# A list of steps made anew, with fillers only into idle PSUM banks

## The chip, the cores and the metric

The kernel runs on one core of one Trainium2 chip. The metric is the device time of one execution in microseconds (us). The core has a matrix engine (TensorE, PE in the profile, with its weight loads as PEld), a vector engine (VectorE, DVE), a scalar engine (ScalarE, ACT), GpSimd (POOL) and a queue engine (SyncE, SP) that only issues DMAs here. TensorE writes into PSUM, which has eight banks; VectorE and ScalarE read it from there.

## The reference

Two blocks follow each other. The first is a delta-rule recurrence over 768 steps for 4 batches of 8 heads with a state of 48 x 48 each:

```python
k_n = k / (np.linalg.norm(k, axis=-1, keepdims=True) + 1e-06)
for t in range(S):
    y[:, :, t] = np.einsum('bhd,bhde->bhe', q[:, :, t], state)
    v_old = np.einsum('bhde,bhd->bhe', state, kt)
    state = state + bt[:, :, :, None] * np.einsum('bhd,bhe->bhde', kt, vt - v_old)
```

Its output, with the heads side by side (4 x 768 x 384), goes through a layer norm and a two-layer MLP with a residual:

```python
xn = (x - mu) / np.sqrt(var + 1e-06) * g_ln
ch = np.maximum(xn @ w_ch1, 0.0) @ w_ch2
return (x + ch).astype(np.float32)
```

All is 32-bit floating point. The first weight is 384 x 1536, the second 1536 x 384.

## The kernel before

The 768 steps are cut into 12 chunks of 64. Within a chunk the recurrence becomes matrix products: a Gram matrix of the keys (`gram`, products L821, copies L842 by ScalarE, then a DMA to DRAM named `gd`), the inverse of a triangular matrix made from it, a product of that inverse with the corrected values (`recur`, L1035 and L1059 or L1090; for chunk 0 L1071), the output (L1097) and the new state (L1107). For chunk 0 the inverse is made on TensorE (`first_inverse`): after one multiply by -beta (L745) come five stages, each with two products E (L773, one per half of the heads, 32 small matmul records each), a predicated copy of them by VectorE (L778), two products Z (L788), and then VectorE's transposes (L737) and ScalarE's copies (L731) of Z. For the later chunks the inverse is made by rows on VectorE (`rows_inverse`, pairs of L909 and L916), between a read of the Gram blocks from DRAM and a write and read of the result through DRAM, and two halves are joined on TensorE (L946, L951, L983, L989). Keys and queries of the first chunks are transposed on TensorE (`first_kt`, L630, with ScalarE's copies L635).

Each chunk's output goes through a layer norm (L1141 to L1153, the root on ScalarE at L1147), is transposed (L1185 for the first chunks), and enters the MLP of that chunk (`mlp`). Chunk 0 takes the plain form: 24 tiles of the first layer (L1408, six matmul records each, relu by ScalarE at L1416) and then the second layer (L1450). Chunk 1 uses L1428; later chunks use a form with fewer products (L1309) and the second layer a form with seven products (L1525). The weights arrive as 64-bit words that ScalarE, VectorE and GpSimd turn into 32-bit floats (L586, L591, L594, L604) in the start of the run.

All of it is recorded first as steps, each with its engine, an estimated cost, a function that issues it and the keys it reads and writes (`Line.add`), from which its dependencies follow. A long text `ORDER` then lists the numbers of all steps, and `Line.emit` issues them in that order; `in_this_order` makes every engine keep it. An `f` in the list is a filler: one matmul of a zeroed tile `nought` with 256 columns, whose result nobody reads (`zeros`, L1603, two matmul records), written always into the upper half of the PSUM tile f0. There are 21 of them, all ahead of the MLP's first tile. Three more fillers are ordinary steps: `fill` (L619), 512 columns each, into the PSUM tile f3 at the very start. The PSUM tiles are `two` and `by` (two banks each) and f0 to f3 (one bank each).

Of the kernel before, what the change touches and what calls it, by code (L numbers as in the profile page):

```python
# [16 lines left out]
C = 64  # L17
# [32 lines left out]
class Step:  # L50
    __slots__ = ("eng", "cost", "fn", "deps", "n", "name", "key", "plan")


class Line:
# [6 lines left out]
    def __init__(self):  # L61
        self.steps = []
        self.filler, self.fill_after = None, ()
        self.writer = {}
        self.readers = {}
        self.tag = "first"

    def add(self, eng, cost, fn, r=(), w=(), name="", after=(), **plan):
        s = Step()
        s.eng, s.cost, s.fn, s.n, s.name, s.plan = eng, cost, fn, len(self.steps), name, plan  # L70
        s.key = f"{self.tag} {eng} {name or next(k if isinstance(k, str) else k[0] for k in w)}"
        deps = set()
        for k in r:
            if k in self.writer:
                deps.add(self.writer[k])
        for k in (*w, *after):
            if k in self.writer:
                deps.add(self.writer[k])
            deps.update(self.readers.get(k, ()))
        for k in r:  # L80
            self.readers.setdefault(k, []).append(s)
        for k in w:
            self.writer[k] = s
            self.readers[k] = []
        deps.discard(s)
        s.deps = deps
        self.steps.append(s)
        return s

    def emit(self, tc):  # L90
# [6 lines left out]
        made = tc.nc.cur_bb.bb.instructions  # L97
        for w in ORDER.split():
            if w == "f":
                self.filler[0]()  # L100
                continue
            a, b = (w.split("-") * 2)[:2]
            for s in self.steps[int(a) : int(b) + 1]:
                assert s not in done and s.deps <= done, s.key
                n = len(made)
                s.fn()
                done.add(s)
                if s.eng == "DVE" and s.plan.get("port"):
                    shared = made[-1]
                if s.eng == "Pool" and "bulk" not in s.plan and shared is not seen:  # L110
                    tc.add_manual_dep(
                        made[n], shared.name,
                        mybir.DependencyInfo(mybir.DependencyClass.Sync, mybir.DependencyReason.DATA),
                        reason="shared port",
                    )
                    seen = shared
# [15 lines left out]
66 8 47 257 6 9-11 1 12 41-44 48-49 7 13 15 0 5 2 65 60 39 256 40 55 53-54 56 52 58-59 57 64 86 85 79 35 78 80 37-38  # L132
77 70 96 75 81 89 74 90 88 91 33 97 87 71 3 14 16 98-100 32 101 26 4 17 105-106 73 72 82 104 84 50 18 23 83 102 92
313 63 108 36 107 69 250 124-125 30 129 216 103 29 93-95 126 109-112 51 76 118-119 122 128 27 31 120 19 f f 133 115
130 114 410 314 409 404 401 113 316 411 315 406 68 407 261 264 403 67 327 260 263 262 265 414 328 266 413 259 326
408 325 412 131-132 134 230 121 123 127 f f 141 135 117 248 144 116 238 209-210 20 142 21-22 136 143 137 24-25 239
147-148 249 138 146 139 145 140 149 234 246 151 156 154 150 231 28 152-153 157 251 163 244 228 160 213 226 155 161
224 215 214 164 211-212 158-159 f f f f f 165 162 232 240 168 172 166-167 45 61 662 62 664 217 241 169-170 174 220
178 317 180-181 319 218 171 173 175-176 245 182 247 179 177 f 183 185 318 369 190 267 415 320 184 227 219 191 196
222 363 321-322 195 370 34 268-271 221 46 258 229 272 193 186 273 187 f 197 329 189 188 323 331 194 192 274-281 198  # L140
282 f f 330 199 283 200 284-285 235 286-289 223 290-291 f 201 205 242 236 243 332 364 333 206-208 203-204 202
334-335 339 337 292-294 665 233 225 237 666 661 674 676 416 400 338 f 341 343 371 254 340 295-299 345 300-303 346 f
361 372 362 349 365 350 366 f f 435 342 344 351 347 434 437 436 252 f 438 253 348 439 355 405 324 336 402 304 476
474 477 309 475 312 306 308 791 307 310 790 305 311 793 367-368 473 352 356 373 357-358 353 374 255 354 f f 440 575
359 577 360 478 576 601 578 581 602 376 607 579 582 375 479-481 418 585 419 580 586 387 420 608 583 589 584 590 587
593 421 417 482 399 678 668 484-485 442 486-496 382 588 594 377 379 597 591-592 613 595 388 381 596 598 422 497 423
378 498 424-425 614 428 599 603-604 426-427 619 675 663 667 677 673 679-680 380 609 394 600 620 429 605 638 431 441
610 430 433 393 432 443 606 383 389 444-445 611 615 499 669 483 500-510 681 511-515 390 516-517 384 518-519 448 446
639-640 447 385 616 612 391 449-450 397 670-671 395 1075-1076 1088 392 386 453 451-452 520 454 521 621 617 522-524
396 1078 398 469 1077 1080 1079 1087 924-925 795 792 788 794 796-797 787 525 798 526 672 682 618 683 641 623 642 624  # L150
643-645 625-626 646 627-628 647-648 629-630 527-528 653 529-530 458 622 455 531 456 532-533 457 461 799 534-535 654
536 459 537-541 460 542-543 659 544 465 631-634 649 684 689 687 932 688 686 928 931 545-547 655 934 548 926 690-693
463 462 466 468 464 467 550 552 551 549 933 936 1181 1184 1182 935 1183 938 937 656 694 697 650 829 833 685 696 789
471 1081-1082 635 800 698 830 801 835 699-701 834 836 839 831 841 840 842 702-704 657 705-709 803 710-711 553
712-714 802 554 557 832 555 558 556 847-848 837-838 715 1083 716-717 564 718 658 719 660 720-721 1550 1549 1089 856
930 1552 1090 853-855 559 862 843 563 561 560 562 804 565 722-725 939 726 845 805 566 844 808 810 809 846 568 567
569 813-814 811 863 806 864-867 859-860 470 807 812 818-819 727-728 857 869 940 868 815 729 851 849-850 852 941 730
820 731 816 732 817 733-736 570 825 942 821 571 574 573 822 826-827 823-824 828 572 879 889 880 872-873 881-883
874-875 884 943 1551 1554 858 870 737 944 738-745 695 746-759 945-946 1179 1187 651 1180 652 636-637 1189 1186 927
1191 929 1190 1188 1193 760 1192 876 890-892 877 947-949 1084-1085 1092 1091 1093 1555 1094 861 871 888 886-887 893  # L160
878 897-900 1095 885 901 894-895 1096 902 980 472 1194 903 1097 915 896 972 950-951 981 764 762 1086 1098 761 763
1100 1195 904-905 916 906-909 975 917-918 910 982 986 973 978 1562 1099 919 1375 1101-1102 1376 1103 954-955 952
1196 920 1197 921 987 1185 912 911 1556 979 992 1563 974 1553 1564 765-766 776 1199 984 983 993 769 768 959 985 1104
767 953 956 770 1105-1108 1111 1110 1112-1113 957 1114-1117 960 1118-1125 958 1126-1129 961 1130 1561 1566 988 990
771 1198 991 996 989 997 772 998 994 999 774 1565 1567 1004 1007 1568 1005 995 775 1010 1008 1006 1009 963 1131-1132
773 1133-1134 1013-1017 1200 777-779 1201 1135-1136 1109 962 1000 1018 1001 781 1019 1002 1030-1031 1003 780 1011
1032 1204 782 1023 1033 1024-1027 1034 1021 1020 1040 1012 922 1377 1655 1378 1380 913 923 1381 914 1382 1369 1657
1370 1654 1379 1653 1372 964 1371 1368 1137-1138 977 1022 1227 1139 1383 1140 1557 1141 1035 1142-1143 1028 1202
1041-1043 1144 966 1661 965 1373 967-968 1228 1038 1037 1231 1029 1203 1145 1044 1048 1045 1049-1050 1384 1146 1036
1046 1147 1385 1051 1055 1052-1053 1056 1386 1057-1058 1148 1047 1374 1229 1149-1150 1054 783-784 970-971 969 786  # L170
1205 1207 1206 785 1151 1388 1039 1235 1246 1232 2038 1059 1066-1068 1060 1387 1389 1152 1209 1153 1061 1154-1156
1390 1236 1069-1070 1237 1157-1158 1071 1250 1063 1242 1159-1160 1072 1391 1247-1248 1239-1240 1278 1062 1254 1230
1238 1243-1244 1251-1252 2040 1255 1288 1269-1270 1210 1392 1161 1569 976 1208 1214 1253 1245 1558 1266-1267 1162
1241 1249 1163-1165 1215 1256 1263 1257 1166 1258 1167 1211-1212 1168 1559 1216 1169 1213 1570-1571 1218 1170-1172
1264 1271 1265 1268 1259 1272 1260 1274 1273 1275 1279 1173 1217 1276 1280-1281 1261 1393 1658 1663 1665 1656 1662
# [75 lines left out]
def kernel(  # L251
# [13 lines left out]
    nc = tc.nc  # L265
# [1485 lines left out]
```

## Time and profile before

| | us |
|---|---|
| three timed executions | 528.7, 529.7, 532.6 |
| median | 529.7 |
| profiled execution, from first to last instruction (its span; no other time of it is recorded) | 530.0 |
| TensorE busy | 497.3 |
| VectorE busy | 353.4 |
| GpSimd busy | 281.9 |
| ScalarE busy | 208.4 |
| fillers at L1603, 42 matmul records, from 16.8 to 75 us | 14.7 |
| fixed fillers at L619, 6 matmul records, from 9.2 to 13.2 us | 4.0 |
| first matmul of the first MLP layer (L1408) starts at | 76.4 |

A row in order of time gives the start and the duration in us, the engine, the line of the kernel, the operation, what it writes and reads, the shapes, how many equal instructions it stands for, and in square brackets how long the engine had been idle before and what ended that. A row by stretch gives the stretch and its length, then for TensorE, its weight loads, VectorE, ScalarE and GpSimd the busy time with the number of instructions, then the share of TensorE's full clock that was granted, the busy share of the DMA engines and the GB/s that they moved.

### The profile page before, as it was taken

What the parts mean: (1) busy time and instruction counts of PE and PEld (TensorE: products, weight loads), DVE (VectorE), ACT (ScalarE), POOL (GpSimd) and SP (SyncE); (2) the same over time, 40 slices, a digit from 0 to 9 for tenths busy, and PEclk for the clock granted to TensorE, in tenths of its full rate; (3) what the DMA queues carried; (4) which work ended last, traced back from release to release, by engine and by line L of the source; (5) the groups of instructions that cost most, each with busy time, mean ns of one, the idle gap of its engine ahead of it and who ended that gap; (6) DMA issues with size and microseconds to landing.
All of it is one profiled execution on the core that took longest, in us unless ns stands there. A gap on an engine that the chain in (4) does not pass through costs nothing.

```text
span 530.0 us, 22859 instructions
## 1 busy us (share of the span) xinstructions
PE 497.3 (94%) x10014; PEld 454.8 (86%) x10014; DVE 353.4 (67%) x819; ACT 208.4 (39%) x463; POOL 281.9 (53%) x447
## 2 busy tenths in 40 slices
PE   4677898999999999999999999999999999999997
PEld 2565678867889889989999999999999999999996
DVE  4565577788987389996999854988835535344141
ACT  5565473732452242342261451441533413524130
POOL 6033367253365948858665646355375262644644
PEclk9879799999999999999999999999999999999999
DMA  8767657578363846288253366240465312002011
GB/s 192 205 137 119 193 111 181 152 157 149 55 119 72 186 95 144 39 202 170 53 111 47 74 172 131 56 99 6 91 145 84 89 33 76 19 33 60 6 26 30
DMA packets 181635, 54.56 MB, mean 103 GB/s; under 512 B 164888, under 2 KB 177312, under 8 KB 181536
## 3 DMA queue, kind: packets, MB, share of 16 engines
q1 hardware_dynamic: 168512, 40.10, 36.5%
q10 hardware_dynamic: 10816, 9.83, 6.3%
q0 software_dynamic: 2208, 3.17, 3.8%
q8 instruction: 78, 1.28, 1.0%
q14 instruction: 21, 0.17, 0.1%
HBM read 36.30 MB, written 16.78 MB: 100 GB/s over the span
## 4 chain that ended last, share of the span: by engine, by line
PE 75%; DMA 7%; DVE 6%; SPq 5%; issue 3%; POOL 2%; ACT 1%; ACTq 0%; DVEq 0%; POOLq 0%
PE f L1525 27%; PE f L1309 21%; SPq L403 5%; PE f L1428 4%; PE two L821 3%; PE f L1450 3%; PE f L1408 2%; DMA tb<-in_q_dram 2%; PE by L1035 2%; PE two L1035 2%; PE by L1097 2%; DVE tmp L909 2%; DVE xb L916 2%; PE two L1090 1%; PE two L1107 1%
## 5 line engine op out<-in xcount | busy, mean ns | idle before, releaser
L1525 PE MATMUL f<-w_sb,h_all 128*128 128x192 f32 x396 | 82.9, 330 | 0.0
L1512 POOL TENSOR_TENSOR h_all<-h_all 128x256 f32<-128x256 f32 x99 | 73.0, 753 | 17.0 <-PE f L1525 6.8
L1525 PE MATMUL f<-words,h_all 128*128 128x192 f32 x396 | 78.4, 329 | 0.0
L1332 DVE TENSOR_TENSOR h_all<-f,h_all 128x512 f32<-128x512 f32 x72 | 48.9, 686 | 35.1 <-PE f L1309 31.6
L1550 POOL TENSOR_TENSOR words<-h_all 128x128 f32<-128x128 f32 x66 | 30.9, 492 | 70.7 <-ACT h_all L1336 52.2
L1525 PEld LDWEIGHTS f<-w_sb,h_all 128*128 128x128 f32 x396 | 65.1, 190 | 1.1
L1525 PEld LDWEIGHTS f<-words,h_all 128*128 128x128 f32 x396 | 65.1, 190 | 0.6
L909 DVE TENSOR_TENSOR tmp<-xb,gb 128x31 f32<-128x31 f32 (+19 forms) x139 | 54.3, 391 | 4.5 <-POOL xb L896 1.8
L916 DVE TENSOR_TENSOR xb<-xb,tmp 128x31 f32<-128x31 f32 (+19 forms) x139 | 52.2, 375 | 3.0
L1327 ACT COPY h_all<-f 128x512 f32<-128x512 f32 x45 | 26.1, 587 | 69.4 <-PE f L1309 52.4
L403 POOL DMA_DIRECT2D tb<-in_k_dram x64 | 41.6, 655 | 13.5 <-DVE tmp L909 7.6
L1336 ACT ACTIVATE h_all<-h_all 128x512 f32<-128x512 f32 x54 | 32.5, 626 | 29.4 <-DVE h_all L1332 29.2
L1309 PE MATMUL f<-x_new,w_sb 128*128 128x128 f32 x288 | 40.9, 278 | 0.0
L1309 PE MATMUL f<-xnt,w_sb 128*128 128x128 f32 x288 | 40.7, 278 | 0.0
L1543 DVE TENSOR_TENSOR o<-f,x 128x192 f32<-128x192 f32 x33 | 11.6, 350 | 39.2 <-PE f L1525 26.4
L1309 PEld LDWEIGHTS f<-x_new,w_sb 128*128 128x128 f32 x288 | 37.1, 191 | 0.6
L1309 PEld LDWEIGHTS f<-xnt,w_sb 128*128 128x128 f32 x288 | 36.7, 191 | 0.5
L604 POOL TENSOR_TENSOR w_sb<-words 128x768 uint32<-128x768 uint32 (+1 forms) x11 | 15.0, 1375 | 39.6 <-ACT xt L731 24.3
L1428 PE MATMUL f<-xnt,w_sb 128*128 128x256 f32 x144 | 34.1, 385 | 0.0
L1135 ACT COPY x<-by 128x384 f32<-128x384 f32 x23 | 10.5, 480 | 52.6 <-DVE o L1543 25.3
L1428 PEld LDWEIGHTS f<-xnt,w_sb 128*128 128x128 f32 x144 | 26.5, 190 | 3.8
L1525 PE MATMUL f<-w_sb,words 128*128 128x192 f32 x132 | 26.2, 328 | 0.0
(255 smaller groups left out, 1013.4 us busy)
## 6 DMA issues: line engine op xcount, KB each, us to landing
words<-in_moe_w_ch_dram ACTq DMA_DIRECT2D x20, 384.0 KB, 4.5
gd<-gsb SPq DMA_DIRECT2D x11, 512.0 KB, 4.5
v<-in_v_dram SPq DMA_DIRECT2D x24, 192.0 KB, 4.0
kr<-in_k_dram SPq DMA_DIRECT2D x46, 96.0 KB, 3.6
out_dram<-o SPq DMA_DIRECT2D x46, 96.0 KB, 2.5
xld<-xlt SPq DMA_DIRECT2D x9, 384.0 KB, 2.8
xnt<-xld SPq DMA_DIRECT2D x36, 96.0 KB, 2.8
tb<-in_q_dram SPq DMA_DIRECT2D x40, 64.0 KB, 3.3
```

The costliest lines, as they stand in the source:

```text
L403: add(eng, cost, lambda: QUEUE[eng].dma_start(out=out_, in_=in_), r, w, bulk=n * ns / 16e3, np=n, **kw)
L909: lambda j=j, n=n, w=w, t=t: nc.vector.tensor_tensor(out=t, in0=xv[:, 0:n, j : j + 1].to_broadcast([128, n, w]), in1=gv[:, j : j + 1, j + ...
L916: "DVE", dve(n * w), lambda t=t, rest=rest: nc.vector.tensor_tensor(out=rest, in0=rest, in1=t, op=ALU.subtract),
L1035: nc.tensor.matmul(dst[half(e), hp, j], src[drows(hp), (e if n else key_half(c, hp, e)) * GP + j], s_all[drows(hp), e, j], start=(n == 0 o ...
L1309: nc.tensor.matmul(wide(p[:, f : f + 128]), w[:, f : f + 128], r, start=start and i == 0, stop=True, skip_group_check=True)
L1327: add("ACT", act(512), lambda: nc.scalar.copy(o, p), pk, ok)
L1332: add("DVE", dve(512), lambda: nc.vector.tensor_tensor(out=o, in0=x, in1=y, op=op), [*xk_, *yk], ok)
L1336: add("ACT", act(512), lambda: nc.scalar.activation(o, o, ACTF.Relu, scale=scale), [], ok)
L1428: nc.tensor.matmul(p[:, 0:TOK], w1_sb[:, t, f * 128 : (f + 1) * 128], xnt[:, t], start=(t == 0), stop=(t == KC - 1))
L1512: add(eng, cost, lambda: e.tensor_tensor(out=out_, in0=x, in1=y, op=op), r, w, port=2 if eng == "Pool" else 1, pr=-2)
L1525: lambda f=f, t=start and f == order[0]: nc.tensor.matmul(p[:, 0:D2], lhs(f), rhs[:, f], start=t, stop=(f == order[-1]), skip_group_check=True
L1550: lambda f=f + i: e.tensor_tensor(out=s3[f], in0=one(0, 0)[0](f), in1=one(1, 0)[0](f), op=ALU.subtract),
```

## The change

The fixed fillers and the tile `nought` are gone, and so is the memset of it. A filler is now a matmul of the identity tile with 256 columns of it, and it goes into the bank that the next TensorE step of the list writes. `Line.add` notes which step begins a value in a bank (`opens`) and which reads it last (`shuts`), and `emit` keeps a count of live values by bank and stops the build where a filler would fall on one. The list itself is new: it was made under the rule that ScalarE and VectorE take turns where they read one PSUM bank. It holds three fillers instead of 21: one ahead of each of the two first E products and one beside the first MLP tile. The steps and their dependencies are otherwise the same; all numbers in the new list shift, because four steps are missing. The order is changed on every engine: no long run of either list stands in the other.

```diff
         self.steps = []
-        self.filler, self.fill_after = None, ()
+        self.filler = None
         self.writer = {}
         self.readers = {}
+        self.unread = set()
...
+        s.out = w[0] if w else None
+        s.opens, s.shuts = [], []
+        for k in (*r, *(k for k in w if k in self.unread and k not in r)):
+            if k in self.writer:
+                self.writer[k].opens.append(k[:2])
+                s.shuts.append(k[:2])
+        self.unread.difference_update(r)
+        self.unread.update(w)
...
+        order = []
         for w in ORDER.split():
-            if w == "f":
-                self.filler[0]()
+            a, b = (0, -1) if w == "f" else map(int, (w.split("-") * 2)[:2])
+            order += self.steps[a : b + 1] or [None]
+        nxt = None
+        for n in range(len(order) - 1, -1, -1):
+            if order[n] is None:
+                order[n] = nxt.out
+            elif order[n].eng == "PE":
+                nxt = order[n]
+        live = {}
+        for s in order:
+            if isinstance(s, tuple):
+                assert not live.get(s[:2]), s
+                self.filler(s)
                 continue
...
-    c_dve(lambda: nc.vector.memset(nought, 0.0), 0.2, ["nought"], pr=-300)
...
-    def zeros():
-        nc.tensor.matmul(f_[0][:, 256:512], nought, nought[:, 0:1].to_broadcast([128, 256]))
-
-    line.filler = (zeros, 0.44, "f0")
-    for _ in range(3):
-        fill(1, 512, f_[3], FK[3], pr=-100)
+    banks_of = {("two", b): two[:, b] for b in range(2)} | {("by", b): by[:, b] for b in range(2)} | {(f"f{i}", 0): f_[i] for i in range(4)}
+
+    def idle(key):
+
+        nc.tensor.matmul(banks_of[key[:2]][:, 0:256], ident, ident[:, 0:1].to_broadcast([128, 256]))
+
+    line.filler = idle
```

In the start the list changes most. TensorE's steps from the first product on, old and new:

```
old: 2 Gram halves of chunk 0, Gram of chunk 1, f f, E1, q^T, E1, q^T, f f, Z1 Z1, queries of chunk 0, E2 E2 Z2 Z2,
     E3, 5 f, E3, Z3 Z3, k^T of chunk 2, E4, f, E4, Z4, k^T of chunk 2, Z4, Gram of chunk 2, f, E5, k^T of chunk 3,
     f f, k^T of chunk 3, E5, f, Z5 Z5, Gram of chunk 3, product with v (2), f, output, f, state, ...
new: Gram half, Gram of chunk 1, Gram half, f, E1, f, E1, Z1 Z1, q^T q^T, E2 E2 Z2 Z2, E3 E3 Z3 Z3, E4, queries of chunk 0,
     E4, Z4, queries, Z4, E5, k^T of chunk 2, E5, k^T of chunk 2, Z5 Z5, Gram of chunk 2, product with v, output,
     product with v, k^T of chunk 3 (2), state, output, Gram of chunk 3, ...
```

## The prediction

> **What bounds the kernel.** I read the page's first part, then the stretches of time, then the order of time where TensorE is not full. The first line gives each engine's busy time:
>
> ```profile
> PE 497.3 (94%) x10014; PEld 454.8 (86%) x10014; DVE 353.4 (67%) x819; ACT 208.4 (39%) x463; POOL 281.9 (53%) x447
> ```
>
> TensorE is the bound, but not everywhere. The same busy times by stage (length, then TensorE, weight loads, VectorE, ScalarE, GpSimd, granted clock, DMA):
>
> ```profile
> 0.00:76.40 76.40, 53.97 (x1388) 41.46 (x1388) 43.72 (x138) 46.44 (x101) 28.74 (x48) 0.89 0.72 164
> 76.40:110.00 33.60, 30.59 (x918) 27.09 (x914) 25.91 (x61) 16.95 (x43) 18.68 (x22) 1.00 0.64 147
> 110.00:300.00 190.00, 188.28 (x3985) 167.73 (x3987) 161.08 (x360) 67.72 (x161) 119.37 (x172) 1.00 0.55 111
> 300.00:530.00 230.00, 224.45 (x3745) 218.54 (x3736) 122.67 (x262) 77.34 (x159) 115.11 (x207) 1.00 0.31 69
> ```
>
> The first layer of the first MLP starts at 76.4 us. From there TensorE idles 3.0 + 1.7 + 5.6 us, 3.9 of the last after its final matmul. Before it, TensorE is busy 54.0 us, of which 14.7 are the fillers of L1603 (their row in this stretch, x42) and 4.0 the fixed fillers of L619 (9.23 to 13.2): 35.3 us of work in 76.4. So whatever moves the start of the MLP moves the end by as much, as long as the other engines keep pace. In the start the chain runs through the inverse of chunk 0 (five stages of two products E, L773, and two products Z, L788). These rows, in order of time, carry the estimate:
>
> ```profile
> 23.09 1.09 PE L630 MATMUL f<-ident,tb 128*128 128x128 f32 x4 [3.75 <-DMA tb<-in_q_dram]
> 24.11 1.13 PE L773 MATMUL f<-qt,gsb 64*64 64x64 f32 x32
> 25.96 0.71 DVE L778 COPY_PREDICATED gsb<-u,two 128x512 f32<-128x512 int32 x1
> 26.08 1.91 PE L1603 MATMUL f<-u 128*128 128x256 f32 x4
> 27.92 1.05 PE L788 MATMUL f<-xt,gsb 64*64 64x64 f32 x32
> ...
> 39.25 0.77 DVE L737 STREAM_TRANSPOSE qt<-two 128x256 f32<-128x256 f32 x2
> 40.06 0.36 ACT L731 COPY xt<-two 64x256 f32<-64x256 f32 x1 [1.05 <-DVE qt L737]
> ...
> 51.02 1.15 PE L821 MATMUL f<-kt 48*64 48x64 f32 x62 [2.99 <-ACT kt L635]
> 54.02 1.11 PE L630 MATMUL f<-ident,tb 128*128 128x128 f32 x4
> 56.08 2.08 PE L1603 MATMUL f<-u 128*128 128x256 f32 x4 [0.95 <-ACT xt L731]
> 58.94 0.92 PE L773 MATMUL by<-qt,gsb 64*64 64x64 f32 x32
> 64.04 0.68 PE L1071 MATMUL two<-v,xt 64*64 64x48 f32 x32 [0.48 <-ACT xt L731]
> ```
>
> The row at 40.06 also shows that two readers of one PSUM pair take turns already: ScalarE waits 1.05 us for VectorE's transposes of the same tile. The change adds no such wait; it lists the steps with that turn in mind.
>
> **The change part by part.** All steps and their dependencies are the same but for four that go (a memset, three fixed fillers). What moves is the list, hence every engine's order. I follow the start.
>
> *Fixed fillers* (L619, 9.23 to 13.2 us). Behind them stand the transposes of chunk 1's k (13.04) and the eight small products of beta (14.00), whose copies (14.37 to 14.83) end ahead of the scaling by -beta (14.86) that the first multiply (15.13) needs. Without them the first chunk's products follow the copy of k^T that ends at 12.04, not at 14.23, and the multiply can start at about 13.6: 1.5 us gained, nothing if chunk 1's k, whose landing the rows do not show, comes late.
>
> *Transposes of q.* In the old list they stand between the two E products of stage 1. TensorE waits 3.75 us for q, works 1.09, and the second E starts at 24.2 although its last operand, VectorE's transpose, ended at 20.2. In the new list both E and both Z of stage 1 come first: 4.0 us. The wait itself is not moved elsewhere: q landed by 23.1, and TensorE reaches the transposes at about that time.
>
> *Fillers ahead of Z1.* They hold TensorE from 26.3 to 28.0, while the operand of Z1 (VectorE, 25.96 + 0.71) is there at 26.7: 1.3 us.
>
> *Order on VectorE in stage 3.* The second Z of stage 2 ends at 36.5 and its transposes start at 39.25, behind a predicated copy and two multiplies by the mask (0.64 each) of chunk 0's queries. In the new list the transposes come first and the multiplies move behind stage 4: 2.7 us. The five fillers at 37.3 only covered this.
>
> *Stage 5.* The last Z of stage 4 ends at 47.9; the product with v (L1071) of the last pair comes at 64.0, 16.1 us later. TensorE stands behind the Gram product of chunk 2 (2.99 us for ScalarE, which itself waits 2.75 for a DMA at the head of chunk 1's inverse), then behind chunk 3's transposes and two fillers. The new list puts stage 5 ahead of all these. Priced by stage 4: 4.7 us from its first E (43.26) to the end of its last Z, 1.1 for the transposes before it (0.77 and the handover), 2.3 for the six copies at the end (61.69 to 63.97): 8.1, so 8.0 gained. But ScalarE's list still holds seven other pieces among these copies (two copies of k^T of 0.59, conversions of 0.56, 0.92 and 0.56, two of 0.2): 3.6 us if none fits in a gap. Between 4.4 and 8.0 I take 6.5.
>
> *From there to the MLP* (64.0 to 76.4, 12.4 us). The new list moves two copies of k^T and two of a Gram block (0.59 each) on ScalarE between the product with v and the first root of the layer norm, and the state's copy too. The old list had the four done by 65.0. 2.4 us if all are on the chain, 0 if none: I take 2.5 lost, with the handovers.
>
> *The clock.* Three fillers stay, two at stage 1 and one beside the MLP's start. Each now writes the bank of the next product, so it waits for that bank's readers as the product would, and cannot fill such a wait. Prices at half clock: an E product 1.06 to 1.13 us (24.11) against 0.69 at full clock (the one at 18.64), 0.37 more. Without the fixed fillers the full clock that the old run had from 11.7 to 21.9 may not come: two products and eight transposes on the chain, 1.7 us. One later spell of half clock more, as long as the old one of 6.8 us, meets five links: 1.8. Together 3.5; bounds are 0 and the third rival. How little idling costs the clock is seen in three neighbouring stretches:
>
> ```profile
> 28.75:32.20 3.45, 2.33 (x140) 2.06 (x134) 2.76 (x10) 2.52 (x7) 0.00 (x0) 1.00 0.95 241
> 32.20:35.60 3.40, 1.62 (x78) 1.34 (x78) 2.67 (x7) 3.32 (x7) 0.67 (x1) 1.00 0.73 130
> 35.60:39.00 3.40, 3.38 (x54) 3.00 (x55) 1.56 (x3) 2.98 (x10) 3.40 (x5) 0.50 0.53 87
> ```
>
> 68% busy is followed by full clock, 48% by half, and a full stretch brings it back. The Trainium skill (TensorE: Matmul & The Clock Gate, Part 1) says that an idle window of about 3.4 us throttles the clock. By that rule the new start, with no pause so long after the first products, would lose nothing and the sum would be 516.5; the rows above disagree, since 48% was enough, so I keep the 3.5.
>
> Sum: 1.5 + 4.0 + 1.3 + 2.7 + 6.5 = 16.0 gained, 3.5 + 2.5 lost: the MLP starts 10 us earlier, at 66. The profiled span is 530.0, 0.3 above the median of 529.7; no other time of that execution is recorded, so the span stands for it: **520 us**.
>
> Is it kept behind the start? For every TensorE step I added up the VectorE time (durations of this trace) that the list puts up to its latest need there, and took off the TensorE time ahead of the step. The old list has at most 16.9 us near 110 us of TensorE work and 13.6 near 190; the new one 12.3 and 3.7. For ScalarE the two lists differ by under 3 us behind the start. So VectorE, 85% busy between 110 and 300, has to be less far ahead, and a TensorE that comes 10 us earlier still finds its operands.
>
> **The rivals.**
> *The gain isn't kept* (527). The first rows' inverse of chunk 1 ends its VectorE part at 68.7 in the old run, and its result is back through two DMA hops at 82.1, 13.4 us later; the queue of SP between is nearly unbroken. In the new list that VectorE work stands behind chunk 0's product with v, so it gains less than the MLP does, and chunk 1 may come late and leave TensorE without work around 75 to 110, where it idled 3.0 us. Price: 7 of the 10 us. Against it: fourteen MLP tiles (0.72 each) now stand ahead of chunk 1's first join, seven before.
> *More* (512): the clock holds, stage 5 gains all 8.0, the stage behind it loses nothing: 3.5 + 1.5 + 2.5 more. Against it: ScalarE's 46 busy us in the old start leave little room in 64.
> *Slower* (536): the clock stays at half from the first products to the MLP, because links of 0.7 us with VectorE and ScalarE between them keep each window under the busy share that frees it. 35.3 us of work at 0.37/0.69 more is 19 us, 15.5 beyond what I took. It decides against the change from 13.5 us on. For it: 18 of 21 fillers go. Against it: slowed products are longer, so the share rises, and the fuller list leaves shorter pauses.
> *That it doesn't do what it says*: three fillers at 0.6 to 1.06 us cannot cost over 3.2 us, inside the range.
>
> **Chances.** The forecast (515 to 525) 0.55, not kept 0.20, more 0.12, slower 0.13. Runs of this kernel differ by 0.7%, so 1% (5.3 us) is about the least that can be told from no change. Faster by over 1%: 0.66; within: 0.21; slower: 0.13. The range 511 to 531 takes in the bounds of stage 5, of the stage behind it and of the clock as far as it costs 14 us, and leaves out the slower rival and the end of "more".
>
> **What will show it.** The first MLP matmul (L1408 of before) near 66; the second E of stage 1 at about 20 and no wait for q; the product with v near 50; granted clock from 10 to 60 us at half for about 20 us; TensorE idle below 4 us from the MLP's start to 110. It is wrong if ScalarE or SP stands behind a weight or k load in the new order, which the list alone doesn't show, if the clock is at half throughout, or if chunk 1 comes late.

## The result, and the profile after

The changed kernel takes 537.7 us (median of four runs, 536.5 to 538.1) against 529.9 for the kernel before beside it (528.7 to 532.6): a ratio of 1.0135, with a 95% interval of 1.0106 to 1.0163. It is slower by 7 to 8 us; the forecast was 520, some 10 faster than before. The profiled execution has a span of 536.3, 6.3 above before.

First part of the page of the changed kernel, and its stages by the same columns as before (the first ends where the first MLP tile starts):

```profile
PE 495.0 (92%) x9972; PEld 457.2 (85%) x9972; DVE 359.7 (67%) x818; ACT 208.7 (39%) x463; POOL 280.4 (52%) x447
```

```profile
0.00:65.60 65.60, 43.19 (x1281) 36.62 (x1281) 38.45 (x134) 43.38 (x96) 22.14 (x40) 0.90 0.79 180
65.60:110.00 44.40, 37.63 (x1040) 33.34 (x1043) 29.37 (x64) 20.03 (x49) 22.83 (x27) 0.88 0.61 137
110.00:300.00 190.00, 183.81 (x3817) 164.27 (x3810) 156.17 (x334) 64.33 (x153) 117.23 (x171) 0.99 0.54 109
300.00:536.30 236.30, 230.36 (x3849) 222.99 (x3847) 135.69 (x288) 81.00 (x166) 118.19 (x210) 1.00 0.30 68
```

The start is 10.8 us shorter (10 had been forecast). Behind it TensorE idles 6.8 us in the second row (3.0 before) and 6.2 in the third (1.7 before), and the granted clock of the second row fell from 1.00 to 0.88. In order of time, TensorE's rows of the start:

```profile
16.95 1.98 PE L817 MATMUL f<-kt 48*64 48x64 f32 x64 [3.08 <-ACT kt L632]
...
20.86 1.13 PE L769 MATMUL f<-qt,gsb 64*64 64x64 f32 x32
...
23.08 1.13 PE L769 MATMUL two<-qt,gsb 64*64 64x64 f32 x32
23.98 0.99 PE L784 MATMUL by<-xt,gsb 64*64 64x64 f32 x32
...
44.58 0.69 PE L769 MATMUL by<-qt,gsb 64*64 64x64 f32 x32
...
51.27 0.65 PE L1067 MATMUL by<-v,xt 64*64 64x48 f32 x32
...
65.76 1.16 PE L1404 MATMUL f<-xnt,w_sb 128*128 128x128 f32 x6
```

The last product E of stage 5 starts at 44.6 (58.9 before), the last product with v at 51.3 (64.0) and the first product of the MLP at 65.8 (76.4).

The list of TensorE's waits (engine, bank, line, what ended the wait: us in total, times, longest) shows what is new:

```profile
PE by L947 <- issue: 3.3, 1, 3.3
...
PE two L1103 <- issue: 2.3, 2, 1.7
PE two L817 <- issue: 2.0, 1, 2.0
PE f L784 <- issue: 1.9, 1, 1.9
```

"issue" means that TensorE stood still and waited for no semaphore. I numbered all of TensorE's records (LDWEIGHTS, MATMUL and the few semaphore records) in order of start. Each of these stops comes at a number that leaves 193 when divided by 256, in both traces: 8 stops of over 0.15 us, 4.3 us in all, before; 14 stops, 15.5 us, after. The same remainder holds for all such stops in every later trace of this study. (In before's list of waits the same word stood, with 1.1 us at most.) The page's part on DMA queues has their source:

```profile
q8 instruction: 78, 1.28, 1.0%
```

78 packets of 16 KB for 20,083 records: one for every 257. **TensorE's instruction stream arrives in blocks of 256, and each stop ends 1.2 to 1.6 us after such a packet has landed.** The Trainium skill (Runtime: NRT & Kernel Launch, Instruction fetch mechanics) states the same block, 16 KiB or 256 instructions, fetched while the block before it executes, and calls the cost of crossing to the next "mostly hidden". The trace agrees with the block and not with the cost. A block is 128 matmul records with their weight loads. 64 small ones take 1.1 us at full clock (the Gram product at 47.16), so 128 can be gone in 2.2 us, and the next block takes longer to come.

The largest stop, chunk 1's second join product, cuts its group of 128 records in two:

```profile
77.79 1.29 PE L942 MATMUL f<-xnj,gsb 32*32 32x32 f32 x128
79.01 1.60 PE L1404 MATMUL f<-xnt,w_sb 128*128 128x128 f32 x12
80.54 0.60 PE L947 MATMUL by<-xt,es 32*32 32x32 f32 x46
84.45 0.90 PE L947 MATMUL by<-xt,es 32*32 32x32 f32 x82 [3.31 <-issue]
```

The same place by stretches of 3.4 us (columns as above):

```profile
78.20:81.60 3.40, 2.94 (x160) 2.67 (x148) 2.82 (x10) 2.22 (x4) 2.38 (x5) 1.00 1.04 338
81.60:85.00 3.40, 0.55 (x64) 0.55 (x66) 0.00 (x0) 0.22 (x1) 1.84 (x2) 1.00 0.47 91
85.00:88.40 3.40, 3.29 (x104) 2.90 (x94) 2.97 (x5) 0.55 (x2) 1.00 (x1) 0.68 0.02 5
88.40:91.80 3.40, 3.40 (x50) 3.11 (x45) 3.16 (x9) 2.13 (x7) 2.99 (x5) 0.50 0.76 158
```

The packet of this block started only at 82.1, 3.8 us behind the crossing at 78.3, and until 81.6 the DMA engines were full (share 1.04). TensorE then stood nearly a whole stretch, and behind it the clock was at half from 86.2 to 93.0, although TensorE was busy 3.29 and 3.40 us of the last two stretches. Before, four MLP tiles lay between the two join products, and the stop there was 0.28 us:

```profile
84.07 2.94 PE L1408 MATMUL f<-xnt,w_sb 128*128 128x128 f32 x24
86.95 0.54 PE L951 MATMUL by<-xt,es 32*32 32x32 f32 x38
87.77 0.96 PE L951 MATMUL by<-xt,es 32*32 32x32 f32 x90 [0.28 <-issue]
```

To see the whole, I split each TensorE step's time, from its start to the next one's, into stops, other waits and the rest. The rest I compare with the shortest that the same step took in any run of this study; what is above that is "longer products". Behind the first MLP tile, in us:

| | before | after | difference |
|---|---|---|---|
| first MLP tile starts | 76.4 | 65.6 | -10.8 |
| steps at their shortest | 419.4 | 420.5 | +1.1 (one more product falls behind the tile) |
| longer products | 24.1 | 31.5 | +7.4 |
| stops without a wait | 3.7 | 11.3 | +7.6 |
| other waits, with the 3.9 at the end | 5.9 | 6.8 | +0.9 |

Together +17.0 and -10.8: 6.2 of the 6.3 us. Of that growth of the longer products, 5.6 us lie from 80 to 120 and from 200 to 220 us, where the granted clock is 0.81 to 0.85 right behind the stops that end at 84.5, 105.9 and 204.8. Behind the first tile the clock was at half for 13.6 us in all (86.2 to 93.0, 106.7 to 110.1, 205.7 to 209.1); in the kernel before it never was.

### The profile page after: what moved, and what is told of

Read it like the earlier page. It is cut to its first block, busy times and chain, and to the rows that moved or that the text cites. A ratio compares the mean times of both kernels' runs of the same rounds, so it can differ in the third digit from the quotient of the medians.

```text
span 536.3 us, 22820 instructions
## 1 busy us (share of the span) xinstructions
PE 495.0 (92%) x9972; PEld 457.2 (85%) x9972; DVE 359.7 (67%) x818; ACT 208.7 (39%) x463; POOL 280.4 (52%) x447
## 4 chain that ended last, share of the span: by engine, by line
PE 86%; issue 5%; DVE 3%; ACT 3%; DMA 2%; SPq 0%; ACTq 0%; DVEq 0%
PE f L1521 29%; PE f L1305 22%; PE f L1424 6%; PE two L817 4%; PE f L1404 3%; PE f L1446 3%; PE by L1031 2%; PE by L1093 2%; PE two L1103 2%; PE two L1031 2%; PE two L1086 2%; DMA words<-in_moe_w_ch_dram 2%; ACT xt L728 1%; PE f L817 1%; PE by L979 1%
## 5 line engine op out<-in xcount | busy, mean ns | idle before, releaser
L1328 DVE TENSOR_TENSOR h_all<-f,h_all 128x512 f32<-128x512 f32 x72 | 49.3, 686 | 30.4 <-PE f L1305 18.6
L1521 PEld LDWEIGHTS f<-words,h_all 128*128 128x128 f32 x396 | 66.7, 194 | 1.8 <-issue 1.1
L1546 POOL TENSOR_TENSOR words<-h_all 128x128 f32<-128x128 f32 x66 | 29.4, 467 | 73.9 <-ACT h_all L1332 23.2
L912 DVE TENSOR_TENSOR xb<-xb,tmp 128x31 f32<-128x31 f32 (+19 forms) x139 | 55.9, 402 | 3.4
L905 DVE TENSOR_TENSOR tmp<-xb,gb 128x31 f32<-128x31 f32 (+19 forms) x139 | 55.4, 399 | 3.3
L1332 ACT ACTIVATE h_all<-h_all 128x512 f32<-128x512 f32 x54 | 33.0, 628 | 24.0 <-DVE h_all L1328 23.5
L1539 DVE TENSOR_TENSOR o<-f,x 128x192 f32<-128x192 f32 x33 | 11.5, 351 | 31.8 <-PE f L1521 19.7
L609 POOL TENSOR_TENSOR w_sb<-words 128x768 uint32<-128x768 uint32 (+1 forms) x11 | 14.8, 1352 | 24.1 <-ACT x L1131 12.6
```

Source lines behind the costliest of these rows:

```text
L905: lambda j=j, n=n, w=w, t=t: nc.vector.tensor_tensor(out=t, in0=xv[:, 0:n, j : j + 1].to_broadcast([128, n, w]), in1=gv[:, j : j + 1, j + ...
L912: "DVE", dve(n * w), lambda t=t, rest=rest: nc.vector.tensor_tensor(out=rest, in0=rest, in1=t, op=ALU.subtract),
L1328: add("DVE", dve(512), lambda: nc.vector.tensor_tensor(out=o, in0=x, in1=y, op=op), [*xk_, *yk], ok)
L1332: add("ACT", act(512), lambda: nc.scalar.activation(o, o, ACTF.Relu, scale=scale), [], ok)
L1521: lambda f=f, t=start and f == order[0]: nc.tensor.matmul(p[:, 0:D2], lhs(f), rhs[:, f], start=t, stop=(f == order[-1]), skip_group_check=True
L1546: lambda f=f + i: e.tensor_tensor(out=s3[f], in0=one(0, 0)[0](f), in1=one(1, 0)[0](f), op=ALU.subtract),
```

## The experiments

Ratios are to the kernel before, run beside on the same chip. "Tiny products" are products of a 16x16 corner of the identity with one column, two records with a weight load each, so four instructions. A count of stops always goes by the number in the stream.

### The same list, with the count shifted

```diff
+            if first and not isinstance(s, tuple) and s.eng == "PE":
+                first = False
+                self.pad()
...
+    def pad():
+        for _ in range(36):
+            nc.tensor.matmul(f_[2][0:16, 0:1], ident[0:16, 0:16], ident[0:16, 0:1])
```

This is the first of three kernels; the other two have 24 and 20 in place of 36, and the last has them in the kernel before.

> The changed kernel with 36 tiny products of the identity (16x16 by one column, into a bank that is written later) ahead of TensorE's first product, where it waits for the keys until 6.9 us anyway. They are 144 instructions (72 LDWEIGHTS, 72 MATMUL), so every 256th instruction of the stream falls on a product 144 instructions earlier; nothing else moves. Theory F: the sum of stops without a wait falls from 15.4 us to 8 or 9, the 3.3 us at the join of chunk 1 and the 2.0 at the Gram product of chunk 4 go or move, and the time falls by 3 to 7, to 531 to 535. Theories C and R: no change beyond 1 us, 537 to 538.

> The same with 24 tiny products, 96 instructions. Theory F: by the instruction times of the trace this is one of the worst places for the boundaries, the stops grow from 15.4 to 18 to 24 us, and the time rises by 2 to 8, to 540 to 546, above the kernel with 144. Theories C and R: 537 to 538, the same as with 144.

> The kernel before with 20 tiny products, 80 instructions, ahead of TensorE's first product, its list untouched. Theory F: the old list's boundaries happen to lie well (4.3 us of stops); 80 instructions on they lie at their worst, 10 to 14 us, and the time rises by 4 to 9, to 534 to 539. Theories C and R: no change beyond 1 us, 529 to 531.

| | ratio | stops ahead of / behind the first tile | span |
|---|---|---|---|
| changed, 144 instructions more | 1.0040 (1.0005 to 1.0076) | 6.1 / 6.0 | 531.6 |
| changed, 96 more | 1.0101 (1.0064 to 1.0138) | 7.6 / 6.7 | 534.8 |
| before, 80 more | 1.0210 (1.0165 to 1.0255) | 3.0 / 8.5 | 542.7 |

All stops sit at 193 in the new numbering, so they moved with the count: the stop at the Gram product of chunk 4 is gone in the first, and others stand at Gram products near 48 and 59 us. Nothing of the work changed, and the new list's time fell by 4.5 to 5 us in one kernel, against 1.0124 and 1.0135 unshifted, and the old list's rose by 11. Three expectations on the count failed: with 144 the stops came to 12.1 us and not 8 or 9 (the time, 534.0, was in its range); with 96 the stops came to 14.3 and not 18 to 24, and the time did not rise (540 to 546 expected), its interval overlaps that of the list unshifted; and the kernel before rose to 542.9 where 534 to 539 was expected, with stops inside their range. Where the stops fall is foretold by the count, how long they are only roughly. The kernel before is the clearest. Its tiny products cost 1.2 us themselves, as the identity is ready only at 7.47 there; to these come 7.1 us more of stops and 5.6 more of longer products behind the first tile. (The three add up to 13.9, where the span grew by 12.7.) Its join, unmoved, now has the stop, one record before its end:

```profile
89.19 1.28 PE L955 MATMUL by<-xt,es 32*32 32x32 f32 x127
94.02 0.26 PE L955 MATMUL by<-xt,es 32*32 32x32 f32 x1 [3.54 <-issue]
```

So the old list owed part of its time to where its boundaries fell.

### The stop by itself

```diff
         line.emit(tc)
...
+        run(256, 1)
+        run(128, 64)
...
+        run(320, 1)
+        run(96, 128)
```

`run` issues so many products of so many columns. Beside the first two the DMA engines carry little (share 0.05 and less from 536 to 560 us); what is left out ahead of the third starts nine loads of 0.79 MB into free tiles.

> The changed kernel with products appended behind its last one, to measure the stop by itself: 256 tiny products of the identity (512 matmul records, 1024 instructions, by 1 column) with no transfer under way, 128 of 64 columns, then nine loads of a weight piece (0.79 MB each, into tiles that are no longer needed) and 320 tiny products at the same time, then 96 products of 128 columns. Theory F: in the first part TensorE stops at every 256th instruction without a wait, from one resumption to the next takes 3.0 to 4.0 us however fast the products are; beside the loads 4.5 to 6.5 us; with 128 columns (128 records of over 0.05 us) no stop. Rival: the stops belong to the places where they were seen (bank changes, weight tiles) and not to the count; then none here, or at other spacings.

TensorE's rows (L1721 is the line of the appended products):

```profile
532.46 41.29 PE L1721 MATMUL f<-ident 16*16 16x1 f32 x768 [0.52 <-DVE o L1539]
...
579.39 3.56 PE L1721 MATMUL f<-ident 16*16 16x1 f32 x128 [1.16 <-issue]
583.68 3.56 PE L1721 MATMUL f<-ident 16*16 16x1 f32 x128 [0.73 <-issue]
588.25 3.57 PE L1721 MATMUL f<-ident 16*16 16x1 f32 x128 [1.00 <-issue]
```

The clock was at half here, and 128 records of tiny products took 3.56 us. With next to no transfers that was enough for the next block: no stop in 512 records and their loads, with 3.3 to 3.7 us from crossing to crossing, where stops were expected. Beside the loads the same products stopped after every 128th record, with 4.3 to 4.7 us from one resumption to the next (4.5 to 6.5 expected). With 64 or 128 columns there was no stop. So the stops belong to the count and the pace, not to banks or tiles, and a block comes in at most 3.7 us on a quiet chip and in 4.3 to 4.7 beside loads. In the kernels, from one crossing to the resumption behind the next, it was 2.2 to 4.1 us where the DMA engines had been under 0.1 busy in the 2 us ahead of the packet, and 3.3 to 7.8 where they had been over 0.9 busy.

### Chunk 1's join

Two tiles moved between the join products; and, in another kernel, four weight loads moved behind the join (steps 372, 371, 384 and 383, from where the first line below has them to behind step 420). A third run repeats the changed kernel beside them.

```diff
-... 372 589 603 590-591 593 371 604 384 592 383 415 594-595 609 416 596 417 ...
+... 372 589 603 590 371 604 384 383 415 591 593 592 594-595 609 416 596 417 ...
```

> The changed kernel's list with two tiles of the first MLP layer (six long products each, 1.35 us together) moved from ahead of chunk 1's first join product to between it and the second; their ScalarE copies move with them. Nothing else moves, the boundaries keep their count. Theory F: the 256 instructions ahead of the stop of 3.3 us then hold two long tiles more, so the stop shrinks by about 1.3, to about 2, and with it some of the half clock behind it: 535 to 537, 1 to 2 us under the changed kernel on the same chip. If the stop belonged to the join itself (its operands or its bank), it stays at 3 or over and the time stays.

> The changed kernel's list with the four weight loads that ScalarE's queue issues from 75.2 to 77.8 us (0.38 MB each) moved behind chunk 1's join, some 8 us later. Theory F with a fetch that stands in line with the data transfers: the fetch issued near 78 us comes after 4.0 to 4.8 us instead of 6.2, the stop at the join falls from 3.3 to 1.2 to 2.0 us, and the time by 1 to 3. Rival: the fetch has its own way and a slow one is chance; then the stop stays at 3 or over. The loads come later, so a conversion of weights could come late further on; that would show as a wait of TensorE for w_sb or words behind 110 us.

> The changed kernel itself, unedited, on the same chip as the three others, for comparison, and to see how far its stops vary from one execution to the next: 1.010 to 1.016 of the kernel before; the stop at chunk 1's join between 2.5 and 4 us, the sum of stops 13 to 18 us.

The second join product with the tiles between, and then with the loads moved:

```profile
81.43 2.94 PE L1416 MATMUL f<-xnt,w_sb 128*128 128x128 f32 x24
84.30 0.60 PE L959 MATMUL by<-xt,es 32*32 32x32 f32 x46
85.57 0.90 PE L959 MATMUL by<-xt,es 32*32 32x32 f32 x82 [0.67 <-issue]
```

```profile
83.69 0.90 PE L959 MATMUL by<-xt,es 32*32 32x32 f32 x82 [0.72 <-issue]
...
88.25 0.45 PE L991 MATMUL f<-xnj,gsb 32*32 32x32 f32 x30 [1.57 <-issue]
```

The changed kernel again: ratio 1.0124 (1.0084 to 1.0164), a stop of 2.93 at the join. With the tiles spread: 0.67, less than the 2 us expected, and the time is 534.1 against 536.3, ratio 1.0081 (1.0049 to 1.0113); the two intervals overlap, so the gain in time is not shown. With the loads moved: 0.72 as well, and the packet started 0.85 us behind the crossing instead of 3.4 to 3.8, so the loads were what delayed that block; but the loads now fill the DMA engines from 85 to 94 us (share 0.94 to 1.09), beside the next two blocks, whose stops are 1.57 and 1.45 (none of over 0.15 in the changed kernel), and the time does not fall by the 1 to 3 us expected (1.0143, 1.0113 to 1.0173). Moving transfers moved the stop; longer products between the short ones shrank it and left 0.76 and 0.63 at the next two.

### New start with the old rest, and old start with the new rest

The steps up to the first MLP tile in one list's order, the remaining ones in the other's.

> The changed kernel's list up to the first MLP tile (with its three fillers), and behind it the remaining steps in the order of the old list. Theory F (instruction fetch: TensorE stops at every 256th instruction of its stream, LDWEIGHTS and MATMUL each counted, whenever the 256 before went by in less than the time that a fetch takes; the start's gain is real and was eaten by 11 us more of such stops and their follow-ups): the first MLP tile near 66, no long wait for chunk 1's inverse behind it, stops of 4 to 9 us in all (from the two traces' instruction times put together, with a fetch taken at 3.9 to 4.4 us), so 515 to 522. Theory C (the gain of the start cannot be kept, because chunk 1's rows come late whatever list stands behind): TensorE waits for the inverse of chunk 1 around 80 to 90, 525 to 530. Theory R (the new start costs its time later by a slower clock): 528 to 534 with the granted clock under 0.9 behind 70 us.

> The kernel before with its own list up to the first MLP tile (all 24 fillers), and behind it the remaining steps in the changed kernel's order. Theory F, with a model fitted to the runs so far (the fetch is asked for 32 instructions ahead of a boundary, comes 3.8 us later, more beside transfers): the boundaries lie badly, stops of about 17 us in all, the largest at chunk 1's join, at the Gram product of chunk 4 and near 218, and the time about 545 (540 to 550). If the new rest is slower by itself: 545 too, so this run counts only beside the next. If the loss belonged to the new start: 530.

> The same with 28 tiny products (112 instructions, under 1 us) right behind the first MLP tile, the place that the same model calls the best: stops of 5 to 6 us in all, and the time about 10 us less than without, 532 to 538. If the rest is slower by itself and the count does not matter: 541 to 550, a little above the kernel without the 28.

| | ratio | first tile | behind it: longer products / stops / waits |
|---|---|---|---|
| new start, old rest | 0.9975 (0.9941 to 1.0008) | 70.0 | 31.4 / 3.6 / 7.6 |
| old start, new rest | 1.0326 (1.0272 to 1.0380) | 79.8 | 32.4 / 9.8 / 6.3 |
| the same, 112 instructions more | 1.0218 (1.0159 to 1.0277) | 75.8 | 32.0 / 7.7 / 7.1 |

The new start with the old rest missed its 515 to 522: 531.5. TensorE did not wait for chunk 1's rows. A stop of 2.1 us at 59 and half clock from 60 to 83 us, where no fillers stood, took the gain. That is what theory R had forecast, time and clock: the old rest, too, took 9.9 us longer behind the new start than in the kernel before, 7.3 of them in longer products and none in stops. (Its profiled execution, 535.3 us, was the slowest of the ten, 3.9 above their median.) The old start with the new rest is the slowest of all: behind the first tile it took 14.9 us longer than the kernel before, so most of the loss belongs to the new rest; its tile came 3.4 us late with the same start, with half clock once more from 66.7 to 73.5. The model's two forecasts from the count came out half right. The first time held (540 to 550; 547.9 measured), with 10.0 us of stops and not 17. The second fell by 6 us and not by 10 (542.0 against 532 to 538, which lies in the other theory's 541 to 550), with 9.6 us of stops and not 5 to 6; places where the model had none or little had stops of 1.5 and 1.9 us. Both theories have their share here: the count moved the time, and the new rest has more stops at most places. Behind the first tile it had 6.0 to 11.3 us of them in all runs but the one whose join was both spread and shifted; the old rest had 2.6 to 4.4, and 8.5 with the 80 instructions.

### Holding the clock

Fillers of 256 columns into the upper half of f0 where TensorE waits, and tiny products so that the count comes out at a chosen place.

```diff
 # ORDER, g a filler, p a tiny product; steps 430, 434, 436, 597 are TensorE's waits from 59 to 79 us
-... 430 ... 434 ... 351 ... 436 ... 597 ...
+... g g g p(x11) 430 ... g g 434 ... g 351 ... g g g p(x11) 436 ... g 597 ...
```

This is the new start with the old rest; in the changed kernel nine fillers stand ahead of steps 337, 351, 355, 430 and 434. The kernel of the third text has the tiles and the loads of the join moved as well.

> The changed kernel with 28 tiny products ahead of its first product (112 instructions), and 9 fillers of 256 columns into the upper half of f0 plus 3 tiny products where TensorE waits between 50 and 67 us (48 instructions). Boundaries: a sum of stops of 9 to 12 us instead of 15.4, about 5 of it behind the first MLP tile instead of 10.5. Theory F with the clock as its follow-up: the half clock between 57 and 72 goes too, and the time is 529 to 533. If the clock alone mattered and not the stops: 534 to 536. If neither: 537 to 538.

> The kernel with the new start and the old list behind it, with 32 tiny products ahead of the first product, and, in the waits between 59 and 79 us, 10 fillers into the upper half of f0 and 22 tiny products: 256 instructions in all, so behind them the boundaries lie where they lay without. Theory F with the clock as its follow-up: the half clock from 57 to 82 us of that kernel goes, the stop of 2.1 us at 59 shrinks, and the time falls by 4 to 7 against it, to 0.985 to 0.99 of the kernel before. Theory C (chunk 1's rows come late whatever is done): TensorE waits for them longer by what it gained, and the time is that of the kernel with the new start, 0.995 to 1.0.

> Both of these with the tiny products and the nine fillers of the kernel that held the clock (28 tiny products ahead of the first product, 9 fillers and 3 tiny products between 50 and 67 us). That kernel had a stop of 4.3 us at the join. Theory F: this stop falls to 1 to 2 us, the half clock from 80 to 110 us lessens, and the time goes to 0.99 to 0.995 of the kernel before, 525 to 528. If the pieces do not add up: 1.0, 530.

> The kernel with the new start, the held clock and the old rest again, for a narrower interval: 0.991 to 0.9975 of the kernel before, its stops 5 to 9 us.

| | ratio | first tile | behind it: longer products / stops / waits |
|---|---|---|---|
| changed, held | 1.0009 (0.9976 to 1.0042) | 67.7 | 27.7 / 7.6 / 6.6 |
| changed, held, join spread, loads later | 1.0024 (0.9998 to 1.0050) | 69.3 | 29.3 / 0.2 / 9.5 |
| new start, held, old rest | 0.9945 (0.9915 to 0.9975) | 68.0 | 23.5 / 2.6 / 6.4 |
| the same again | 0.9962 (0.9927 to 0.9996) | 71.0 | 24.5 / 2.9 / 5.7 |

The first row has its expected time (530.6, in 529 to 533) but not its expected stops: 12.2 us in all and not 9 to 12, 7.6 behind the tile and not 5. The kernel of the last two rows beats both: 0.4 to 0.5% faster than before, some 1.7% than the changed one. It gained less than expected (0.985 to 0.99), and its ratio alone would not exclude theory C; its trace does, since both join products start without a wait for chunk 1. Against the same lists without the fillers, half clock behind the tile went from 20.1 us to none, and the longer products from 31.4 to 23.5. Run again, it had the time and the stops expected. Its stage behind the start ran at full clock, with 4.8 us of idling:

```profile
68.00:110.00 42.00, 37.22 (x1082) 32.43 (x1083) 32.33 (x68) 22.11 (x52) 26.53 (x31) 1.00 0.66 153
```

The second row is a miss with a lesson. Its stops behind the start are gone, but my own move made a wait of 2.45 us: TensorE's tile behind the join needed ScalarE's relu, which stood behind a weight conversion that now waited 4.7 us for one of the loads that I had moved. The clock behind that wait was 0.62 and 0.70 (90 to 110 us), at half from 92.3 to 106.0, of which TensorE was busy 13.6 us. The time was 531.4, not 525 to 528. A wait costs the clock as a stop does.

### Without the old fillers

All 24 fillers of the kernel before left out, 24 tiny products ahead of the first step.

> The kernel before without any of its 24 fillers (and without the zeroed tile), 24 tiny products ahead of the first product in their place, so that from the first MLP tile on the boundaries lie where they lay. It prices the fillers of the old list. If they hold the clock as the prediction had it (3.5 us for the chain without them, against 1.5 and 1.3 that they cost): the first MLP tile within 2 us of 76.4 and the time within 1 us of before. If the clock without them stays at half up to the first MLP tile: tile 4 to 10 us later, 534 to 540. If they only take up time: tile 3 us earlier, 526 to 528.

The first tile starts at 77.1, within the 2 us, the ratio is 1.0065 (1.0028 to 1.0101): 3.4 us slower, between the first two theories. The clock was at 0.50 to 0.55 from 20 to 30 and 60 to 80 us, and a stop of 3.07 us came at 61.7. The fillers paid for themselves, with little to spare. How much of the 3.4 is clock and how much stops was not separated.

### The copy that held the first products

```diff
-85-86 101-102 84 94 87 83 104 234 103 77-78 ...
+85-86 101-102 84 94 87 83 104 103 234 77-78 ...
```

> The changed kernel's list with ScalarE's second copy of chunk 1's k^T moved ahead of the first weight conversion, which waits 2.8 us for a load; nothing else. If that copy is what held the start: the Gram product of chunk 1 starts near 13.7 instead of 17.0, the first E product at 18 to 19 instead of 20.9, the first MLP tile 1 to 2.5 us earlier. The boundaries keep their count but meet other transfers, so the whole may keep it or lose it: 533 to 538. If the copy is not on the chain: the first E product at 20.9 still.

> The same move in the kernel with the new start, the held clock and the old rest. Behind the start its stops are few (2.6 to 2.9 us), so a start that is 1 to 2.5 us earlier should be kept: 0.990 to 0.994 of the kernel before, against 0.9945 and 0.996 without. If the start's gain is eaten by stops in the start (3.5 to 4.2 us there): 0.994 to 0.998.

ScalarE of the changed kernel, where step 234 is the row at 15.87 and step 103 the row at 16.32:

```profile
12.52 0.58 ACT L632 COPY kt<-f 128x512 f32<-128x512 f32 x1 [0.94 <-PE f L627]
15.87 0.55 ACT L591 ACTIVATE words<-words 128x384 f32<-128x384 f32 x1 [2.77 <-DMA words<-in_moe_w_ch_dram]
...
16.32 0.58 ACT L632 COPY kt<-f 128x512 f32<-128x512 f32 x1
```

TensorE with the copy moved ahead:

```profile
17.58 0.69 PE L769 MATMUL f<-qt,gsb 64*64 64x64 f32 x32 [1.53 <-DVE qt L757]
...
19.66 0.69 PE L769 MATMUL two<-qt,gsb 64*64 64x64 f32 x32 [0.76 <-DVE qt L757]
...
28.83 0.58 PE L769 MATMUL by<-qt,gsb 64*64 64x64 f32 x9 [3.03 <-issue]
```

Both first products E start 3.3 to 3.4 us earlier. Then the next boundary, at the same instruction, takes 3.03 us where it took 0.56, and the one near 57 us takes 3.44 (0.1 to 2.7 in the other runs of this list); the first tile is at 67.7, no earlier than without. The ratio is 1.0049 (1.0014 to 1.0084), against 1.0124 and 1.0135 without the move in other groups, so something was kept, but not by the start. In the best kernel the move brought nothing: 0.9964 (0.9931 to 0.9997), with 6.8 us of stops in the start instead of 3.5 and 4.2.

## Why the prediction was wrong

**The start was right in its sum, not in every term.** It forecast the MLP at 66 (65.8), the product with v near 50 (49.0 and 51.3). Step by step:

- *Fixed fillers*, 1.5 gained: wrong. The first E starts 2.2 us later (20.9 against 18.6), because ScalarE's copy stands behind a conversion that waits for its load. The prediction had named this as something that the list doesn't show; the run with the copy moved shows it: its first E starts at 17.6, 1.1 earlier than before. The new fillers ahead of the two first E products cost time as well: at half clock they took 1.22 us each (19.71 and 21.93), and the second E, whose last operand from VectorE was there at 22.1, started behind its filler at 23.1.
- *Transposes of q and fillers ahead of Z1*, 5.3: from the first E to the first Z1 3.1 us pass instead of 9.3, so 6.2. The second E came at 23.1, not 20; with the copy moved, at 19.7.
- *VectorE's order*, 2.7: the gain goes from 3.9 at the first Z1 to 6.7 at E4, so 2.8.
- *Stage 5*, 6.5: from 6.1 at the second E4 to 12.8 at the last product with v, so 6.7.
- *To the MLP*, 2.5 lost: 2.1.
- *The clock in the start*, 3.5 lost: the half clock that it named came (both first products E take 1.13 us, where the first took 0.69 before), but no loss of its own remains in this sum. The stops of the start (4.3 us, 0.7 before) are in it too, which the prediction didn't have. So part of the agreement in the start is terms that cancel, which is luck.

**The step that failed** is "Is it kept behind the start?". It added up the operands of VectorE and ScalarE and concluded that "a TensorE that comes 10 us earlier still finds its operands". That is so: waits behind the start grew by 0.9 us. But TensorE also has to find its instructions. The term that the sum lacked is 7.6 us of stops and 7.4 of longer products behind the first tile. That the stops come from the count is shown (the same work at other counts, and the appended products). That the clock falls behind them is shown too: from 20 us to the last product, every stop or wait of TensorE of 2 us or more in any trace of this study has half clock beginning no later than 2 us behind its end. That the half clock makes the longer products is borne out across the kernels:

| behind the first tile, us | half clock | longer products |
|---|---|---|
| before | 0 | 24.1 |
| new start, held, old rest; the same again | 0; 3.4 | 23.5; 24.5 |
| changed, held | 10.2 | 27.7 |
| changed; held, join spread, loads later | 13.6; 13.7 | 31.5; 29.3 |
| new start, old rest | 20.1 | 31.4 |
| old start, new rest; with 112 more | 20.5; 20.5 | 32.4; 32.0 |

The run with stops of 0.2 us shows that a plain wait does the same.

*The rivals.* "Not kept" (527) was right that the gain is lost behind the start, but it still forecast a faster kernel, and its cause was wrong: chunk 1's first join product starts with no wait. "Slower" (536) had nearly the right time by luck: it put half clock into the whole start, and the start was as fast as the main forecast had it; the half clock that cost came behind the first tile. The promised "TensorE idle below 4 us from the MLP's start to 110" was the sign that failed: 6.8. The price of three neighbouring stretches held in part: a stretch that TensorE spent mostly idle (0.55 of 3.40 us, from 81.6) was followed by half clock, as at 48% before; that one full stretch brings the clock back did not hold, neither from 86.2 to 93.0 here nor from 92.3 to 106.0 in the kernel with the loads moved and the clock held.

**What could have been read.** The list of waits of the kernel before had eight waits on "issue", all at one remainder of 256. They summed to only 4.3 us, which is the old list's good luck and not a bound: 80 instructions more made it 11.5.

## What to carry to other kernels

Where small products follow each other, ask how long TensorE takes for 128 matmul records of them, and beside which transfers: under some 3.7 us (4.3 to 4.7 beside the loads of the separate run, up to 7.8 in the kernels) it can run out of instructions, and half clock follows where the stop is 2 us or more. Put long products between short ones, and judge a new order at several instruction counts, since a few tiny products at the front moved the time by 1 to 2% with nothing else changed. "issue" in a list of waits is to be summed like any other wait.

## What the runs showed of the hardware

- The block of 256 instructions (128 matmul records with their loads) comes in at most 3.7 us with nearly idle DMA engines and in 4.3 to 4.7 beside loads; in the kernels up to 7.8 us passed from one crossing to the resumption behind the next. Stops of up to 4.3 us were seen.
- The fetch stands in line with data: with four loads of 0.38 MB moved away, one packet started 0.85 us behind the crossing instead of 3.4 to 3.8, and its stop went from 2.9 to 3.3 us to 0.72, while two new ones of 1.57 and 1.45 came beside the moved loads.
- A stop or a wait of 2 us or more brought half clock for one or more stretches of 3.4 us in every trace here (from 20 us to the last product), for as many as four with TensorE busy throughout (92.3 to 106.0). Behind the first tile the longer products cost about as much again as the stops themselves (7.4 and 7.6 us more than before).
